# Value passes one head group at a time over zero-padded keys, and the last two batches exchanged in the seven products

## Chip, cores and metric

One core of a Trainium2 chip. The metric is device time in microseconds (us) of one execution of the whole kernel. A core has TensorE (PE, matmuls; its weight loads are shown as PEld), VectorE (DVE), ScalarE (ACT), GpSimd (POOL, which issues the input loads here) and SyncE (SP, which issues most stores).

## What is computed

Attention over 8 batches with 12 heads, 448 tokens and a head dimension of 64; its output, as 3584 rows of 768, goes through two matrices with SiLU between them.

```python
scores = scale * np.matmul(q, k.transpose(0, 1, 3, 2))
attn = np.exp(scores - max); attn = attn / sum
attn_out = np.matmul(attn, v)
x = attn_out.transpose(0, 2, 1, 3).reshape(B * S, H * D)   # 3584 x 768
h = x @ w_in                                               # 768 x 2048
g = h * (1.0 / (1.0 + np.exp(-h)))
out = g @ w_out                                            # 2048 x 768
```

## The kernel before

**Units and pairs.** The 12 heads are worked on in groups of 4 (HG). A unit is one group of one batch; batch 0 is cut into two pieces of the queries, so there are 27 units, 0 to 26. Units 0 to 6 stand alone ("lone"). The other twenty form ten pairs (7 and 8, 9 and 10, ... 25 and 26). The 448 keys of a unit lie in four chunks (NCH = 4) of the 128 partitions. In a pair three chunks are full, and the fourth, half a chunk, is shared: the first unit ("low") has its last keys in partitions 0 to 63, the second ("high") in 64 to 127 of one buffer, E[(ns[0], 3)].

**A unit's way.** `scores` (L350) and `scores_rest` multiply keys and queries in row strips (tiles of 32 rows, `score`, L337); `expo` (L374) takes the exponential on ScalarE into buffers E (9 of them, NE). For a pair `add_e` (L385) adds three chunks into T on VectorE, and `attend_sums` (L416) makes the sums of both units in one PSUM bank. `attend` (L424) runs the value passes, part 1 and part 2 (even and odd columns of V), with `attend_mm` (L400) in column strips (tiles of 32 columns; four such matmuls run side by side). For a pair a part takes two banks at once, one for each unit: 24 matmuls over the full chunks, and 8 over the 64 rows of the shared chunk (`rest()`), in tiles of 64 rows. `inverse` (L461 to L475) turns the sums into reciprocals, transposed, and `norm` (L491) writes the normalized output to xT, which frees the bank. Of the PSUM, a ring "m" of 4 banks serves sums, value passes, first products and second products; a ring "s" of 2 serves scores.

**The two matrices.** For batches 0 to 5 `ffn1` (L503, tile h, helper `times`) multiplies by w_in, 6 matmuls for each of 16 slices f; ScalarE's tanh (L529) and VectorE's `gate` (L564) make G. If TensorE's last work was in column strips, `times` does its product in strips too (four matmuls of 32 columns for one of 128), which spares a change of tile shape. The second product runs on quads of 128-row blocks (qd), each in seven products of half size instead of eight (`product`, tile p; sums S on VectorE, L705; `take_copy` L776 and `take_sum` L782 write the output). The first two blocks are multiplied plainly (tile o).

**The last two batches**, 6 and 7 (PB = 6), go through w_in together, in seven products for each f (`pair_product`, L652, tile f). They need four combinations of x (`combine_x`, L611, tile sx) and eight of w_in (`combine_w_in`, L629, tile tw), in buffers that were E's or V's. Product 1 is the first half of row 0 with w_in itself, product 2 its second half, product 5 takes sx_1, the sum of both halves of row 1, with tw_1; product 6 takes sx_2, 7 sx_3, 3 sx_4, and 4 the second half of row 1. Row 0 is batch 6, row 1 batch 7. ScalarE copies (L674) and VectorE adds (L678) gather the results, and ScalarE's Silu (L685) writes G.

**What sets the order.** All instructions are put in order by hand: class `Order` runs a planner at build time with estimated durations, and each engine's instructions are issued in the order in which the planner starts them. For VectorE and ScalarE `step` (L117) chooses among the ready operations the one with the smallest `at + op.bias`, its time of readiness plus a bias: -10 for `inverse` and `norm`, -4 for gates and output sums, -1 for add_e, 0 for S, 4 (SXB) for sx, 4 or 8 (TWB + f0) for tw, 20 for the transposes of keys and queries, 30 for combinations of w_out. On TensorE the loop at the end chooses among scores (`run_qk`), value passes (`run_av`, in the order of av_seq) and products (the list moe); where a score is due within AWAIT, a value pass is held back for it. POOL issues the loads in one fixed order: for each unit keys, queries, and four loads of V (`load_v`, L271), and w_in and w_out among the first. V has two buffers, one batch each; V's loads for a batch wait for the value passes of the batch two before.

Two small pieces that the change replaces:

```python
            4: (x[0, 1], sx_t.get(2), ALU.subtract),   # combine_x
...
        av_seq += [(ns, part) for part in range(3)]
```

Of the kernel before, what the change touches and what calls it, by code (L numbers as in the profile page):

```python
# [16 lines left out]
SWITCH = 0.094  # L17
# [12 lines left out]
def act(n):  # L30
    return n * 0.00087 + 0.13

# [45 lines left out]
class Order:  # L78
# [38 lines left out]
    def step(self):  # L117

        soon = []
        for eng in ("ACT", "DVE"):  # L120
# [45 lines left out]
def kernel(  # L166
# [37 lines left out]
    AWAIT = 0.8  # L204
    FAR = (NT * B // 4 - 3, NT * B // 4 - 1)
    TWB, SXB = 4, 4
# [59 lines left out]
    def load_v(b, hg0, hg1, x):  # L266
# [3 lines left out]
        first, count = X_TOK[form(b, hg0)][x]  # L270
# [315 lines left out]
    def old_buffer(name, home, cols):  # L586

        if home == "V":
            t = sb.tile([128, NH, NCH, D], FP16, name=name, tag="V", bufs=2)
            t = t.rearrange("p h c d -> p (h c d)")  # L590
        else:
# [25 lines left out]
    def combine_w_in(m, f0):  # L617
        if (m, f0) not in tw_t:
            made = old_buffer(f"tw_{m}_{f0}", W_HOME.get((m, f0), "E"), 512)
# [11 lines left out]
    W_HOME = {(1, 0): "V"}  # L631
    PBANK = {1: "A", 6: "A", 7: "A", 4: "A", 2: "B", 5: "C", 3: "C"}

    def pair_product(f, m):
# [6 lines left out]
        x = {(r, i): x3(PB + r, 3 * i) for r in range(2) for i in range(2)}  # L641
        lo, at = f // 4 * 4, slice(128 * (f % 4), 128 * (f % 4 + 1))
        a, w = {
            1: (x[0, 0], w_in_part(0, 0, f, f + 1)),
            2: (x[0, 1], w_in_part(1, 0, f, f + 1)),
            3: (sx_t.get(4), w_in_part(1, 1, f, f + 1)),
        }.get(m, (None, None))
        if a is None:
            i = {4: 4, 5: 1, 6: 2, 7: 3}[m]
            a, w = x[1, 1] if m == 4 else sx_t[i], tw_t[(i, lo)][:, :, at]  # L650
        for c in range(3):
            nc.tensor.matmul(  # L652
                out=pp_t[(f, PBANK[m])],
                lhsT=w[:, c, :],
                rhs=a[:, c, :],
                start=(c == 0 and m in (1, 2, 5)),
                stop=(c == 2),
                skip_group_check=True,
# [25 lines left out]
    def silu(f, r, x):  # L684
        nc.scalar.activation(  # L685
            out=G[:, f, S * r : S * (r + 1)],
# [260 lines left out]
    pair_todo = [(m, f0) for f0 in (0, 4) for m in (1, 2, 3, 4)]  # L947

    def plan_pair():
        while pair_todo and not od.pool:  # L950
            m, f0 = pair_todo[0]
            if (m, f0) in W_HOME:
                if not v_ring.can(1, od.now):
                    return
                v_ring.take()
            elif (m - 1, f0) not in W_HOME:
                if qk_seq or not e_ring.can(1, od.now):
                    return
                e_ring.take()
            pair_todo.pop(0)  # L960
            pair_w[(m, f0)] = od.add(
                Op(
                    "DVE",
                    0.98,
                    lambda m=m, f0=f0: combine_w_in(m, f0),
                    [pair_w[(k, f0)] for k in {2: (1,), 4: (2,)}.get(m, ())],
                    TWB + f0,
                )
            )

    def queue_pair():
        xs = {(r, c): x_op[(PB + r, c, 0)] for r in range(2) for c in range(NDC)}
        v_ring.take()
        e_ring.take(2)
        od.add(
            Op(
                "ACT",
                2.7,
# [590 lines left out]
```

## Time and profile before

Runs: 397.7, 398.45, 398.64 us, median 398.45. The profiled execution took 398.49 us.

| | us |
|---|---|
| profiled execution, its time | 398.49 |
| its span, first to last instruction | 396.7 |
| TensorE busy | 385.3 |
| VectorE busy | 275.1 |
| ScalarE busy | 252.7 |
| POOL busy | 83.7 |
| mean granted TensorE clock | 0.996 |

The span is the time from the first to the last instruction of any engine; the rest of the time lies around it. Busy times overlap. An engine's idle time before an instruction is put down to the engine or DMA whose signal came last ("issue": nothing that the profile shows). In rows of the timeline the first two numbers are the start in the span and the duration; consecutive equal instructions are merged, and a matmul's duration includes its way through the array, so that the next one starts before it ends. "128*32" is the tile, rows by columns. PEclk is the share of the TensorE clock that was granted.

### The profile page before, as it was taken

To read this page: it belongs to the slowest core of one execution; us is meant where nothing else is said; L and a number is where in the kernel's file an instruction comes from. 1 tells how busy PE (TensorE), PEld (TensorE's weight loads), DVE (VectorE), ACT (ScalarE), POOL (GpSimd) and SP (SyncE) were. 2 spreads that over 40 slices of the span, in tenths; PEclk is the share of its full clock that TensorE was granted. 3 is DMA by queue.
4 is the path that set the end of the run, shared out by engine and by line. 5 is a ranking of instruction groups with operands and counts; after the bars stand their busy time and mean duration, and the time that the engine had idled before them with its cause. 6 is when DMAs were issued, how large, how long until landed. Compare 5 with 4: busy or idle time off the path is not lost.

```text
span 396.7 us, 10765 instructions
## 1 busy us (share of the span) xinstructions
PE 385.3 (97%) x4429; PEld 202.3 (51%) x4429; DVE 275.1 (69%) x570; ACT 252.7 (64%) x399; POOL 83.7 (21%) x153
## 2 busy tenths in 40 slices
PE   8998999999999999999999999999999969999995
PEld 6666775444455445544445444444445524555663
DVE  2475776999985489457988469787899584456441
ACT  4986985696862883159675396867867237892120
POOL 7532547206001430024200614041000000000000
PEclk9999999999999999999999999999999989999999
DMA  7999999909033943173603667274000320001333
GB/s 113 204 209 210 159 185 170 184 17 138 5 88 81 132 56 59 49 135 51 96 7 84 109 106 104 36 128 71 2 2 22 89 53 0 0 2 30 92 99 101
DMA packets 35362, 34.54 MB, mean 87 GB/s; under 512 B 11376, under 2 KB 33776, under 8 KB 35312
## 3 DMA queue, kind: packets, MB, share of 16 engines
q0 software_dynamic: 24784, 22.82, 38.5%
q1 hardware_dynamic: 9952, 10.33, 9.7%
q8 instruction: 35, 0.57, 0.6%
q10 hardware_dynamic: 576, 0.69, 0.5%
q14 instruction: 15, 0.12, 0.1%
HBM read 45.61 MB, written 11.01 MB: 143 GB/s over the span
## 4 chain that ended last, share of the span: by engine, by line
PE 96%; DVE 1%; DMA 1%; issue 1%; ACT 0%; DVEq 0%; POOLq 0%
PE p L503 30%; PE h L503 29%; PE s L337 13%; PE a L400 11%; PE f L652 8%; PE o L503 3%; PE a L416 2%; DMA rk<-in_k_dram 1%; PE z L1474 1%; DVE xT L491 0%; DVE p L678 0%; ACT E L374 0%; DVE sx L611 0%; DVE KT L306 0%; ACT u L674 0%
## 5 line engine op out<-in xcount | busy, mean ns | idle before, releaser
L374 ACT ACTIVATE E<-s 128x896 f16<-128x896 f32 (+1 forms) x172 | 149.4, 914 | 31.4 <-PE s L337 29.7
L503 PE MATMUL h<-xT,w_in_t 128*128 128x448 f16 (+3 forms) x1122 | 119.0, 322 | 1.7 <-issue 1.7
L503 PEld LDWEIGHTS <-w_in_t 128*32 128x32 f16 (+1 forms) x1122 | 63.3, 97 | 53.7 <-issue 15.9
L529 ACT ACTIVATE th<-h 128x448 f16<-128x448 f32 (+1 forms) x112 | 54.5, 493 | 30.4 <-PE h L503 21.9
L564 DVE SCALAR_TENSOR_TENSOR G<-th,h 128x448 f16<-128x448 f16 (+2 forms) x112 | 55.5, 509 | 19.3 <-ACT th L529 16.9
L776 ACT COPY ost<-p 128x384 f32<-128x384 f32 x52 | 25.0, 481 | 65.5 <-PE p L503 62.0
L271 POOL DMA_DIRECT2D V<-in_v_dram x88 | 48.6, 573 | 75.9 <-PE a L400 62.1
L503 PEld LDWEIGHTS <-G 128*128 128x128 f16 (+1 forms) x580 | 42.9, 98 | 32.5 <-issue 5.6
L337 PE MATMUL s<-rq,KT 32*128 32x448 f16 (+4 forms) x768 | 50.6, 337 | 0.9 <-DVE rq L324 0.5
L503 PE MATMUL p<-w_out_t,G 128*128 128x384 f16 (+1 forms) x328 | 49.2, 326 | 0.0
L503 PEld LDWEIGHTS <-S 128*128 128x128 f16 (+1 forms) x456 | 30.1, 97 | 22.3 <-issue 3.1
L400 PE MATMUL a<-E,V 128*32 128x448 f16 (+3 forms) x864 | 40.1, 334 | 0.0
L503 PE MATMUL p<-D,S 128*128 128x384 f16 (+1 forms) x232 | 37.0, 326 | 0.0
L256 POOL DMA_DIRECT2D rq<-in_q_dram x27 | 15.2, 564 | 103.3 <-PE s L337 78.5
L491 DVE SCALAR_TENSOR_TENSOR xT<-a,rdn 128x448 f16<-128x448 f32 (+1 forms) x54 | 28.7, 567 | 10.7 <-PE a L400 9.9
L782 DVE TENSOR_TENSOR ost<-p,ost 128x384 f32<-128x384 f32 x39 | 21.5, 553 | 20.4 <-PE p L503 15.1
L337 PEld LDWEIGHTS <-KT 32*128 32x128 f16 (+2 forms) x864 | 17.4, 98 | 28.7 <-issue 26.0
L385 DVE TENSOR_TENSOR T<-T,E 128x1792 f16<-128x1792 f16 x20 | 21.8, 1089 | 13.7 <-ACT E L374 13.6
L400 PEld LDWEIGHTS <-V 128*32 128x32 f16 (+2 forms) x864 | 17.6, 95 | 20.4 <-issue 13.2
L385 DVE TENSOR_TENSOR T<-E,E 128x1792 f16<-128x1792 f16 x20 | 21.7, 1087 | 4.9 <-ACT E L374 4.9
L652 PE MATMUL f<-sx,tw 128*128 128x448 f16 x72 | 18.3, 381 | 3.3 <-DVE sx L611 3.2
L306 DVE STREAM_TRANSPOSE KT<-rk 128x256 f32<-128x256 f32 (+3 forms) x48 | 16.7, 385 | 6.3 <-DMA rk<-in_k_dram 6.1
(67 smaller groups left out, 323.0 us busy)
## 6 DMA issues: line engine op xcount, KB each, us to landing
out_dram<-ost SPq DMA_DIRECT2D x194, 48.0 KB, 1.7
rk<-in_k_dram POOLq DMA_DIRECT2D x24, 224.0 KB, 5.2
rq<-in_q_dram POOLq DMA_DIRECT2D x21, 224.0 KB, 5.4
w_in_t<-in_moe_w_in_dram POOLq DMA_DIRECT2D x6, 512.0 KB, 11.1
w_out_t<-in_moe_w_out_dram POOLq DMA_DIRECT2D x4, 768.0 KB, 13.7
V<-in_v_dram POOLq DMA_DIRECT2D x43, 64.0 KB, 3.8
V<-in_v_dram POOLq DMA_DIRECT2D x40, 48.0 KB, 3.8
out_dram<-ost SPq DMA_DIRECT2D x8, 96.0 KB, 2.1
```

Source lines behind the costliest of these rows:

```text
L271: nc.gpsimd.dma_start(out=VT[b][32 * x : 32 * (x + 1), hs, 0:count, :], in_=v[b, hs].rearrange("h (i g) d -> i h g d", g=TPP)[:, :, first ...
L337: nc.tensor.matmul(out=pS[p0 : p0 + 32 * (x1 - x0), h % 2, at : at + nq], lhsT=KT[(b, hg)][32 * h : 32 * (h + 1), c, x0:x1, :, e], rhs=QT[ ...
L374: nc.scalar.activation(out=E[(n, w)][0:kr, 2 * y : 2 * y + 2, 0:nk], in_=pS_t[(n, w, y)][0:kr, :, 0:nk], func=AF.Exp, scale=attn_scale,)
L385: nc.vector.tensor_tensor(out=T[n], in0=T[n] if step else E[(n, 0)], in1=E[(n, step + 1)], op=ALU.add,)
L400: nc.tensor.matmul(out=a[32 * h : 32 * (h + 1), 0:nq], lhsT=w, rhs=e[k0:k1, h, at : at + nq], start=start, stop=stop,)
L491: nc.vector.scalar_tensor_tensor(out=x3(b, cc)[:, cc % 3, 32 * g0 : 32 * g1], in0=acc[(n, part)][:, 0:nq], scalar=0.5, in1=rdn_t[n].rearra ...
L503: nc.tensor.matmul(out=out[i : i + cut], lhsT=w[:, i : i + cut], rhs=x, start=start, stop=stop, skip_group_check=True,)
L529: nc.scalar.activation(out=th, in_=h_t[(b, f, t0)][:, 0 : t1 - t0], func=AF.Tanh)
L564: nc.vector.scalar_tensor_tensor(out=dst[:, f, at + lo : at + hi], in0=th_t[(b, f, t0)][:, lo - t0 : hi - t0], scalar=1.0, in1=h_t[(b, f, ...
L652: nc.tensor.matmul(out=pp_t[(f, PBANK[m])], lhsT=w[:, c, :], rhs=a[:, c, :], start=(c == 0 and m in (1, 2, 5)), stop=(c == 2), skip_group_ ...
L776: nc.scalar.copy(out=ost(qd, *OUT[m]), in_=bank(qd, BANK[m]))
L782: nc.vector.tensor_tensor(out=t, in0=bank(qd, BANK[m]), in1=t, op=ALU.add)
```

## The change

- **Value passes.** `attend` now does one unit and one part at a time, in one bank, with four chunks of 128 rows. The shared chunk is read whole, with both units' keys, and V holds zeros in the half that is not the unit's: `load_v` sets this half of chunk 3 to zero on POOL ahead of the first of the four loads (20 such memsets). av_seq lists the passes as part 1 and 2 of the first unit, then of the second.
- **Roles of the last two batches.** Row 0 of the seven products is batch 7, row 1 batch 6 (`pair_half`, `silu`'s place in G, the gates' entries). `queue_pair` is called after part 1 of the last unit instead of after its part 2. The combinations are queued by `plan_pair` once every first product of batch 5 is placed, each with a home of its own (HOME): sx_1 and sx_2 in xT's buffers, sx_3 and sx_4 in E's. `pair_product` may run in strips. The load of Silu's table is queued by `plan_silu`.
- **VectorE's and ScalarE's choice** is by rank first: bias -9 or less, then up to 35, then above, and by time and bias within a rank. TWB becomes 40, so the combinations of w_in come last.
- AWAIT becomes 0. A norm's reciprocals may be 0.9 late for a pass instead of 1.2. The first products of batch 0 do not use strips any more.

```diff
+def rank(op):
+    return (op.bias > -9) + (op.bias > 35)
...
-                elif best is None or at + op.bias < best[0]:
-                    best = (at + op.bias, op)
+                elif best is None or (rank(op), at + op.bias) < best[0]:
+                    best = ((rank(op), at + op.bias), op)
...
-    AWAIT = 0.8
+    AWAIT = 0.0
     FAR = (NT * B // 4 - 3, NT * B // 4 - 1)
-    TWB, SXB = 4, 4
+    TWB, SXB = 40, 4
...
-        first, count = X_TOK[form(b, hg0)][x]
+        kind = form(b, hg0)
+        if x == 0 and kind != "lone":
+            lo = 64 if kind == "low" else 0
+            nc.gpsimd.memset(VT[b][lo : lo + 64, hs, NCH - 1, :], 0.0)
+        first, count = X_TOK[kind][x]
...
-    def attend(ns, part):
-        made = []
-        lone = len(ns) == 1
-        if part == 0 and not lone:
+    def attend(ns, part, n):
+        if part == 0 and len(ns) == 2:
             attend_sums(ns)
             return
-        for n in ns:
-            a = ps.tile([128, 512], FP32, name=f"a_{n}_{part}", tag="m", bufs=4)
-            made.append(a)
-            acc[(n, part)] = a
-
-        def rest():
+        acc[(n, part)] = ps.tile([128, 512], FP32, name=f"a_{n}_{part}", tag="m", bufs=4)
+        for c in range(NCH):
+            e = E[(ns[0] if c == NCH - 1 else n, c // per_burst(n))]
             for h in range(HG):
-                for i, n in enumerate(ns):
-                    attend_mm(
-                        made[i], n, part, 3, h, 64 * i, 64 * (i + 1), E[(ns[0], 3)],
-                        part == 2, part == 1,
-                    )
-
-        if not lone and part == 2:
-            rest()
-        for i, n in enumerate(ns):
-            for c in range(NCH if lone else NCH - 1):
-                for h in range(HG):
-                    attend_mm(
-                        made[i], n, part, c, h, 0, rows_of(n, c), E[(n, c // per_burst(n))],
-                        c == 0 and (lone or part == 1),
-                        c == NCH - (1 if lone else 2) and (lone or part == 2),
-                    )
-        if not lone and part == 1:
-            rest()
+                attend_mm(
+                    acc[(n, part)], n, part, c, h, 0, rows_of(n, c), e, c == 0, c == NCH - 1
+                )
 
     def inverse(ns, step, i=0):
         g0, g1 = units[ns[0]][2:]
...
+    def pair_half(r, i):
+        return x3(B - 1 - r, 3 * i)
+
     def combine_x(m):
-        if m < 4:
-            made = old_buffer(f"sx_{m}", "V" if m == 3 else "E", S)
-            for i, t in enumerate(made):
-                sx_t[m + i] = t
-        x = {(r, i): x3(PB + r, 3 * i) for r in range(2) for i in range(2)}
+        sx_t[m] = old_buffer(f"sx_{m}", HOME[("x", m)], S)[0]
         a, b, op = {
-            1: (x[1, 0], x[1, 1], ALU.add),
-            2: (sx_t.get(1), x[0, 0], ALU.subtract),
-            3: (x[0, 0], x[1, 0], ALU.subtract),
-            4: (x[0, 1], sx_t.get(2), ALU.subtract),
-        }[m]
+            1: lambda: (pair_half(1, 0), pair_half(1, 1), ALU.add),
+            2: lambda: (sx_t[1], pair_half(0, 0), ALU.subtract),
+            3: lambda: (pair_half(0, 0), pair_half(1, 0), ALU.subtract),
+            4: lambda: (pair_half(0, 1), sx_t[2], ALU.subtract),
+        }[m]()
         nc.vector.tensor_tensor(out=sx_t[m], in0=a, in1=b, op=op)
...
-    W_HOME = {(1, 0): "V"}
+    HOME = {
+        (0, 1): "V", (0, 2): None, ("x", 1): "x", ("x", 2): "x", (0, 3): "E", ("x", 3): "E",
+        (0, 4): "E", ("x", 4): "E", (4, 1): "V", (4, 2): None, (4, 3): "E", (4, 4): "E",
+    }
     PBANK = {1: "A", 6: "A", 7: "A", 4: "A", 2: "B", 5: "C", 3: "C"}
 
-    def pair_product(f, m):
...
         nc.scalar.activation(
-            out=G[:, f, S * r : S * (r + 1)],
+            out=G[:, f, S * (1 - r) : S * (2 - r)],
...
             def run(f=f):
-                strips = od.mode == "cols" and bool(qk_seq or av_seq)
+                strips = b > 0 and od.mode == "cols" and bool(qk_seq or av_seq)
                 op = Op("PE", NDC * mm(t1 - t0), lambda: ffn1(b, f, t0, t1, strips), tail=PE_OUT)
...
     pair_w, pair_x = {}, {}
-    pair_todo = [(m, f0) for f0 in (0, 4) for m in (1, 2, 3, 4)]
+    pair_todo = []
+
+    def xs(r, c):
+        return x_op.get((B - 1 - r, c, 0))
...
+        if "go" not in pair_w:
+            if od.pool or ffn1_left[PB - 1] or (PB - 1, 0) not in x_left:
+                return
+            pair_w["go"] = None
+            pair_todo.extend(HOME)
+        shut = set()
+        for kind, m in list(pair_todo):
+            home = HOME[(kind, m)]
+            mine = pair_x if kind == "x" else pair_w
+            made = [(m,) if kind == "x" else (m, kind)]
...
+            ring = {"V": v_ring, "E": e_ring}.get(home)
+            if None in made or home in shut or (home == "E" and qk_seq):
+                shut.add(home or kind)
+                continue
+            if ring is not None:
+                if not ring.can(1, od.now):
+                    shut.add(home)
+                    continue
+                ring.take()
+            pair_todo.remove((kind, m))
+            if kind == "x":
+                pair_x[m] = od.add(
+                    Op("DVE", 0.9, lambda m=m: combine_x(m), made, SXB)
                 )
+            else:
+                pair_w[(m, kind)] = od.add(
+                    Op("DVE", 0.98, lambda m=m, f0=kind: combine_w_in(m, f0), made, TWB + kind)
+                )
...
+    def plan_silu():
+        made = [g_op.get((PB - 1, f)) for f in range(NFF)]
+        if None not in made and not qk_seq and "silu" not in pair_w:
+            pair_w["silu"] = od.add(
+                Op("ACT", 2.7, first_silu, [x for y in made for x in y], -5)
...
-            g_op.setdefault((PB + r, f + HF * j), []).append(done[(j, r)])
+            g_op.setdefault((B - 1 - r, f + HF * j), []).append(done[(j, r)])
...
-                made = [xs[0, c] for c in (range(3, NDC) if m == 2 else range(3))]
+                made = [xs(0, c) for c in (range(3, NDC) if m == 2 else range(3))]
+                if f > 1 and m in (1, 5):
+                    made.append(xs(0, NDC - 1) and xs(0, 0))
                 i = {5: 1, 6: 2, 7: 3, 3: 4}.get(m)
                 if i:
-                    made.append(pair_x[i])
+                    made.append(pair_x.get(i))
...
-            queue_pair()
...
-        av_seq += [(ns, part) for part in range(3)]
+        av_seq += [(ns, 0, ns[0])] + [(ns, part, n) for n in ns for part in (1, 2)]
...
+                deps += [(x, 0.9) for x in rdn_op.get(n, [None])]
+        at, m = when(deps), m_ring.when(1)
+        return None if at is None or m is None else max(at, m)
...
-        ns, part = av_seq.pop(0)
-        b, hg, g0, g1 = units[ns[-1]]
+        ns, part, n = av_seq.pop(0)
...
+        m_ring.take()
...
-        od.on_pe(op, "rest cols" if two and part == 2 else "cols")
-        if two and part:
-            od.mode = ("rest cols", "cols")[part - 1]
+        od.on_pe(op, "cols")
...
+        if part == 1 and n == NU - 1:
+            queue_pair()
```

More of the change, by code (lines that the diff above doesn't have):

```diff
@@ L590, in old_buffer @@
             t = t.rearrange("p h c d -> p (h c d)")
+        elif home == "x":
+            return [sb.tile([128, 3, S], FP16, name=name, tag="xT", bufs=NX3)]
         else:
@@ L649, in pair_product @@
             i = {4: 4, 5: 1, 6: 2, 7: 3}[m]
-            a, w = x[1, 1] if m == 4 else sx_t[i], tw_t[(i, lo)][:, :, at]
+            a, w = lambda: pair_half(1, 1) if m == 4 else sx_t[i], tw_t[(i, lo)][:, :, at]
         for c in range(3):
[L652 to L658, printed above, removed]
+            times(
+                pp_t[(f, PBANK[m])],
+                w[:, c, :],
+                a()[:, c, :],
+                c == 0 and m in (1, 2, 5),
+                c == 2,
+                strips,
             )
@@ L969, in plan_pair @@
+    def plan_silu():
[3 more added lines that the diff above has]
+                Op("ACT", 2.7, first_silu, [x for y in made for x in y], -5)
             )
     def queue_pair():
[L972 to L978, printed above, removed]
-                first_silu,
-                [x for f in range(NFF) for x in g_op[(PB - 1, f)]],
-                -5,
-            )
-        )
@@ L996, in queue_pair_f @@
-    def queue_pair_f(f, xs):
+            queue_pair_f(f)
+    def queue_pair_f(f):
         done, lo = {}, f // 4 * 4
@@ L1027, in run @@
                     ring.take(need)
-                od.on_pe(op, "full")
+                od.on_pe(op, "cols" if strips else "full")
                 done[m] = op
@@ L1060, in deps @@
                 made += [(done.get(x), 9.0) for x in {2: ["p"], 3: ["u"]}.get(m, [])]
-                return made + (free(0) if m == 1 else free(1) if m == 5 else [])
+                return made + (free(1) if m == 1 else free(0) if m == 5 else [])
             moe.append((deps, int(m in (2, 5)), run, rings))
@@ L1415, in then @@
             def then(at):
-                for _ in range(7 if two else NCH // per_burst(ns[0])):
+                for _ in range((3 + (n == ns[1])) if two else NCH // per_burst(n)):
                     e_ring.give(at)
-                if any(units[n][1] == NG - 1 and units[n][3] == TPP for n in ns):
+                if hg == NG - 1 and g1 == TPP:
                     v_ring.give(at)
@@ L1429, in run_av @@
         else:
-            for n in ns:
-                after_av(n, part, op, nq)
+            after_av(n, part, op, nq)
     def after_sums(ns, op, nq):
@@ L1487 @@
             moe_i, moe_next = moe_ready()
-            av_data["at"] = None
             qk, av = qk_at(), av_at()
-            wait = av_data["at"]
-            if wait is not None and wait <= od.now - 1000 and not (av is not None and av <= od.now):
-                moe_i, moe_next = moe_ready(0)
-                soon.append(min([x for x in m_ring.free if x>od.now] or [od.now+0.1]))
             near = qk_seq and units[qk_seq[0][0][0]][0] == 0 and qk is not None
```

96 lines of the change are left out of this document (31 added, 65 removed).

## The prediction

> **What bounds the kernel now.** I read the page's busy shares first, then its chain, then the list of TensorE's waits, and last the timeline around each wait.
>
> ```profile
> span 396.7 us, 10765 instructions
> ...
> PE 385.3 (97%) x4429; PEld 202.3 (51%) x4429; DVE 275.1 (69%) x570; ACT 252.7 (64%) x399; POOL 83.7 (21%) x153
> ...
> PE 96%; DVE 1%; DMA 1%; issue 1%; ACT 0%; DVEq 0%; POOLq 0%
> ```
>
> TensorE's matmuls are 96% of the chain that ends last, so an edit counts if it changes the number of matmul time slots, the number of times the array changes its tile shape, or TensorE's waits. The list of its waits has six entries. Four are 1.0 us or less and stand in the first 28 us, which the change leaves as they are. The other two:
>
> ```profile
> PE f L652 <- DVE sx L611: 3.2, 1, 3.2
> PE h L503 <- issue: 1.7, 1, 1.7
> ```
>
> The first stands where attention ends and the seven products of the last two batches begin (PE's and DVE's rows of the timeline, start and duration in us):
>
> ```profile
> 318.79 2.44 PE L652 MATMUL f<-xT,w_in_t 128*128 128x448 f16 x12
> 321.43 1.15 DVE L491 SCALAR_TENSOR_TENSOR xT<-a,rdn 128x448 f16<-128x448 f32 x2
> 323.56 0.84 DVE L611 TENSOR_TENSOR sx<-xT,xT 128x1344 f16<-128x1344 f16 x1
> 324.46 5.48 PE L652 MATMUL f<-sx,tw 128*128 128x448 f16 x18 [3.22 <-DVE sx L611]
> 329.77 0.73 PE L652 MATMUL f<-sx,w_in_t 128*128 128x448 f16 x3
> 330.34 0.73 PE L652 MATMUL f<-sx,tw 128*128 128x448 f16 x3
> ```
>
> Four products that need no sum run until 321.2. The next (m = 5) needs sx_1, the sum of both halves of batch 7, and batch 7's last piece is normalized only at 321.4 to 322.5. The wait is 3.22 us, and there is a second loss behind it. From 324.46 to 329.77 eighteen matmuls take 5.31 us. Three of the same shape take 330.34 - 329.77 = 0.567, so 0.189 each, and eighteen should take 3.41. The missing 1.90 us is in the granted clock (PEclk) of the table by stretches:
>
> ```profile
> core 0: us, PE busy (x) PEld busy (x) DVE busy (x) ACT busy (x) POOL busy (x), PEclk, DMA share, GB/s
> 318.00:321.00 3.00, 3.00 (x32) 1.34 (x24) 2.08 (x3) 1.06 (x2) 0.00 (x0) 1.00 0.28 69
> 321.00:324.00 3.00, 0.24 (x2) 0.00 (x0) 3.00 (x6) 0.86 (x2) 0.00 (x0) 1.00 0.32 84
> 324.00:327.00 3.00, 2.54 (x9) 1.14 (x10) 3.00 (x5) 1.31 (x3) 0.00 (x0) 0.67 0.00 0
> 327.00:330.00 3.00, 2.95 (x13) 1.26 (x12) 0.68 (x1) 1.60 (x3) 0.00 (x0) 0.77 0.00 0
> ```
>
> The clock falls to 0.67 and 0.77 right behind the gap and is 1.00 on both sides. The Trainium skill, TensorE: Matmul & The Clock Gate, Part 1, puts the halving of the clock down to an idle window of about 3.4 us and its return to a busy window of that length; by this the loss would be half of 3.4, so an estimated 1.7 instead of 1.90 us, and the sum below would be 0.2 higher.
>
> The second wait is early, in the batch-0 products, which run in strips of 32 columns:
>
> ```profile
> 31.07 0.94 PE L400 MATMUL a<-E,V 128*32 128x224 f16 x32
> 31.84 0.27 PE L503 MATMUL h<-xT,w_in_t 128*32 128x224 f16 x4
> 33.85 1.24 PE L503 MATMUL h<-xT,w_in_t 128*32 128x224 f16 x44 [1.74 <-issue]
> ```
>
> It falls within one product, behind 4 of 48 matmuls, and names no releaser. In this stretch (31 to 33 us) the DMA engines are full and one packet of TensorE's own instructions is among the traffic:
>
> ```profile
> q8 instruction: 1, 0.02, 3.0%
> ```
>
> I read the gap as TensorE having run out of instructions while the next block of them stood in line behind the loads.
>
> **The change part by part.** The base is the profiled execution: 398.49 us with a span of 396.7, so 1.79 lie around the span; the median of the runs is 398.45, the same within 0.04.
>
> *Value passes.* Before, a pair of head groups takes 7 slots of 0.189 us a part for both groups: 24 matmuls of 128 rows run four at a time (6 slots) and the 8 short ones of 64 rows run eight at a time (1 slot). Afterwards each group has its own pass of 16 matmuls over 128 rows, 4 slots, so 8 a part. Ten pairs, two parts: 20 x 0.189 = **+3.78**.
>
> *Changes of tile shape.* The price is read from a repeating stretch:
>
> ```profile
> 79.67 0.57 PE L337 MATMUL s<-rq,KT 32*128 32x448 f16 x8
> 80.18 2.44 PE L503 MATMUL h<-xT,w_in_t 128*128 128x448 f16 x12
> 82.56 0.58 PE L337 MATMUL s<-rq,KT 32*128 32x448 f16 x8
> ```
>
> From 79.67 to 82.56 are 2.89 us for 2 + 12 slots (2.65), so 0.24 for two changes; the neighbouring cycle, from 76.79, gives 0.23. I take 0.115 each. In the order of instructions of the two programs the shape changes 234 times before and 206 times after: the 30 into and out of the 64-row value tiles go, and two others come in. 28 x 0.115 = **-3.22**. So the passes nearly pay for themselves. As a check, two parts back to back:
>
> ```profile
> 95.20 3.07 PE L400 MATMUL a<-E,V 128*32 128x448 f16 x64
> 98.09 1.31 PE L503 MATMUL h<-xT,w_in_t 128*32 128x448 f16 x24
> ```
>
> 2.89 us for 14 slots (2.65) and 0.24 for the two inner changes; 16 slots without them are 3.03. Parts that stand alone gain on the next product, which may stay in strips.
>
> *Roles swapped.* sx_1 is now made of batch 6, which is normalized two units ahead of the end. In the new order all 14 products of quads 8 and 9 stand between the last value pass and the first of the seven products; eight matmuls of them take 374.08 - 372.78 = 1.30 us, so 18.2 us of cover for combinations of 0.85 (sx) and 0.95 us (tw). The 3.22 us wait goes, **-3.22**, and with it the slow clock, **-1.90**.
>
> *Batch 0 without strips.* The same slots with a quarter of the instructions. From the waiting product on, the instructions that TensorE had in hand now last through two whole products (2 x 6 x 0.098 = 1.2 us; thirty take 2.98 us at 41.98), a score burst of 0.5 and about three changes of shape: 31.84 + 0.1 + 2.1, about 34.0, when the block (landed by 33.85) is there. Before, this place (the start of h_0_3) was reached at 35.53; I take **-1.63**. The bounds are 0 and -1.74.
>
> *Memsets.* The 20 memsets of 64 x 256 elements stand on POOL ahead of V's loads. No row has one of this size: the lower bound is POOL's memset of one element, 0.10 us, the upper VectorE's 1.09 for an add of 1792 elements; I take 0.3, nearer the small one, 6 us in all. POOL is busy 83.7 of 396.7 us, and TensorE has no wait on V's loads in the list: cost nothing. Uncovered, it would be one memset for each wait, 20 x 0.1 to 1.09 = 2 to 22 us. Behind a memset queue V's four loads and the next keys and queries. The one place where that is tight: the last piece of w_out (POOL sits idle for it until 61.54) is needed near 63.2 afterwards, against 65.4 before; two memsets move its issue by 0.6 and leave about 1 us.
>
> *VectorE by rank, combinations late.* The same operations. The risk is that they bunch: in the 18.2 us behind attention I count 16 sums at 0.34, 6 adds at 0.56, 3 sx at 0.85, 8 tw at 0.9 and 2 gates at 0.7, together 20.0 us (two sums in a row take 0.75 with 0.42 each, so 0.34 from start to start). Three tw (2.7 us) are needed only by the fifth slice, so it just fits. For this and for bank waits between passes I add **+0.3**: the bounds are 0 and 3 (the 20.0 us entirely in the way, with 1 us for a bank).
>
> The sum: 398.49 + 3.78 - 3.22 - 3.22 - 1.90 - 1.63 + 0.3 = **392.6 us**.
>
> **The rivals.**
>
> 1. *The early gap stays.* The cause is not instructions, or their block comes as much later. For it: its row shows "issue", no cause. Against it: it falls in mid-product, where no instruction waits on another engine. It gives 392.6 + 1.63 = 394.2. The Trainium skill, Runtime: NRT & Kernel Launch, Instruction fetch mechanics, holds that fetching is hidden because instructions issue slower than they arrive, and that TensorE holds 2048 of them; by this rule the gap is no fetch and stays. No row here shows the buffer's size.
>
> 2. *The wait moves into the 14 products.* VectorE comes late with the sums of quads 8 and 9, having normalized the last passes and made sx first. For it: the 20.0 us above. Against it: the closing products (355 to 392 us) have the same sums per product without one wait. Three us and a slow clock behind them (1.90 at most) give 392.3 + 3 to 4.9 = 395.3 to 397.2; I say 396.
>
> 3. *Slower: VectorE's normalizing chain is late at each pair.* One bank per pass lets TensorE reach the second, third and fourth pass sooner, and each needs a bank that a norm frees. The chain behind the sums is 0.65 + 0.33 + 1.17 (two transposes) and 0.62 for a norm, 2.77 us; if an add of 1.09 is ahead of it, 3.86. Between a pair's sums and its first pass stand mostly two products and a score burst, 2.8 us, and two passes (1.5) find banks free: 4.3, so it is hidden. At two pairs of the ten (units 11 and 21) a single product (1.3) stands there, and it isn't. It must cost more than 398.49 + 1.2 - 392.6 = 7.1 us to be slower, 0.71 at each of ten pairs; a full add at each gives 10.9, so 403.5 us.
>
> 4. *The gains come in part and the change washes out*: half of rival 3 and the late w_out, 5 to 6 us, 398.
>
> **How the numbers follow.** Forecast 0.58, with a range of its own of 391.2 (changes of shape at 0.13 us, -0.4; no new waits, -0.3; the early gap wholly gone, -0.1; the spread of the runs shown, about -0.5) to 393.8; rival 1 0.14 (394.2), rival 2 0.11 (396), rival 3 0.10, rival 4 0.07. A difference under 0.3% (1.2 us) can't be told from none here. Faster takes the first three: 0.83; same 0.07; slower 0.10. For eight in ten the range runs from 391.2 over rivals 1 and 2 to 397.
>
> **What would show it.** Right: no wait on sx in TensorE's list and a granted clock of 1.00 throughout behind attention; two passes of 16 value matmuls in about 1.5 us; the first 36 us without a wait of 1.7. Wrong: a wait of "a" on VectorE's xT that recurs at each pair (rival 3), one of "p" on S near 300 to 320 us (rival 2), or value passes of more than 0.78 us each in a row.

## The result, and the profile after

The changed kernel takes 394.47 us (median of four runs), beside 398.43 for the kernel before. The ratio is 0.9898, with a 95% interval of 0.9874 to 0.9922, so about 4 us of the forecast 5.9 came. Medians here and below are of all runs; one disturbed run each of four kernels (after; full tiles in batch 0; clock kept up; the fastest without the exchange) is left out of the ratios, and without it these four medians are 394.01, 407.12, 397.17 and 393.97. The profiled execution took 394.92 us.

The page of the kernel after, its first lines and the shares of the chain that ended last:

```profile
span 393.1 us, 10622 instructions
...
PE 384.6 (98%) x4345; PEld 206.3 (52%) x4345; DVE 274.4 (70%) x570; ACT 253.9 (65%) x399; POOL 89.0 (23%) x173
...
PE 95%; DVE 1%; DMA 1%; ACT 1%; issue 1%; DVEq 0%; POOLq 0%
```

TensorE still bounds the kernel. Its five longest waits (engine, line, releaser; us in total, times, longest):

```profile
PE z L1458 <- DVE zeros L227: 1.0, 1, 1.0
PE a L408 <- DVE xT L479: 1.0, 1, 1.0
PE a L408 <- issue: 0.8, 2, 0.5
PE s L345 <- DVE rq L332: 0.5, 1, 0.5
PE p L491 <- DVE ost L773: 0.4, 1, 0.4
```

Both waits that the prediction set out to remove are gone: 3.2 us on sx, and 1.7 us in batch 0. A wait of 1.0 on xT is new, and a small one of a product on an output tile; the other three stand ahead of the first product of batch 0. The clock behind attention, in the table by stretches of the kernel after:

```profile
core 0: us, PE busy (x) PEld busy (x) DVE busy (x) ACT busy (x) POOL busy (x), PEclk, DMA share, GB/s
321.00:324.00 3.00, 3.00 (x18) 1.56 (x16) 2.33 (x3) 2.24 (x6) 0.00 (x0) 1.00 0.39 102
324.00:327.00 3.00, 3.00 (x18) 1.54 (x17) 1.78 (x3) 2.50 (x7) 0.00 (x0) 1.00 0.41 109
```

It is 1.00, where it was 0.67 and 0.77. The early stage (PE's rows of the timeline, kernel after) has no gap within a product any more:

```profile
32.15 0.95 PE L408 MATMUL a<-E,V 128*32 128x224 f16 x32
33.03 1.32 PE L491 MATMUL h<-xT,w_in_t 128*128 128x224 f16 x12
34.29 0.57 PE L345 MATMUL s<-rq,KT 32*128 32x448 f16 x8
```

The new wait, in the timeline of the kernel after, TensorE's and VectorE's rows:

```profile
117.16 1.47 PE L491 MATMUL p<-w_out_t,S 128*32 128x384 f16 x32
118.56 0.58 PE L345 MATMUL s<-rq,KT 32*128 32x448 f16 x8
118.68 0.76 DVE L696 TENSOR_TENSOR S<-G,S 128x512 f16<-128x512 f16 x2 [2.28 <-PE p L491]
119.36 0.62 DVE L479 SCALAR_TENSOR_TENSOR xT<-a,rdn 128x448 f16<-128x448 f32 x1
...
120.13 0.94 PE L408 MATMUL a<-E,V 128*32 128x448 f16 x16 [0.99 <-DVE xT L479]
```

VectorE stands idle for 2.28 us ahead of an S sum, whose buffer is free only when a product (117.16 to 118.6) has read it. Behind that sum in VectorE's order stands a norm whose value pass had ended at 117.3 us and whose bank TensorE's next value pass needs. So the pass waits 0.99 us at the pair of units 11 and 12. Ahead of the 0.44 us wait on an output tile, at 176 us, VectorE had likewise stood idle, for 3.18 us, before an S sum that needed a buffer.

**A measure without the start.** The first product of batch 0 (tile h) starts at 29.49 us in the profile before and at 30.57 after, and between 29.46 and 30.60 in the others, while the loads come in. To compare profiles I take this start off the span: 396.7 - 29.49 = 367.2 before, 393.1 - 30.57 = 362.5 after, a difference of 4.7 us. The last column of the next table is this number.

| kernel | median, us | ratio to before, 95% interval | span behind the first product |
|---|---|---|---|
| before | 398.4 to 398.7 | 1 | 367.2 |
| after | 394.47 | 0.9898 (0.9874 to 0.9922) | 362.5 |
| after, once more | 394.31 | 0.9894 (0.9870 to 0.9918) | 362.5 |
| before, full tiles in batch 0 | 407.28 | 1.0196 (1.0161 to 1.0231) | 375.9 |
| before, clock kept up | 397.19 | 0.9969 (0.9951 to 0.9987) | 365.5 |
| before, value passes alone | 395.12 | 0.9914 (0.9888 to 0.9941) | 363.4 |
| before, exchange alone | 395.14 | 0.9925 (0.9899 to 0.9951) | 363.5 |
| after, old value passes | 393.61 | 0.9882 (0.9859 to 0.9904) | 362.0 |
| after, 64-row tiles | 401.98 | 1.0090 (1.0070 to 1.0110) | 370.3 |
| after, strips kept | 395.95 | 0.9939 (0.9915 to 0.9963) | 364.3 |
| after, no rank | 398.07 | 0.9976 (0.9958 to 0.9995) | 365.6 |
| after, four S buffers | 392.59 | 0.9847 (0.9816 to 0.9878) | 361.0 |
| passes and full tiles alone | 393.97 | 0.9886 (0.9857 to 0.9916) | 362.4 |
| the fastest without the exchange | 394.26 | 0.9889 (0.9865 to 0.9912) | 361.6 |

### The profile page after: what moved, and what is told of

Read it like the earlier page. It is cut to its first block, busy times and chain, and to the rows that moved or that the text cites. A ratio compares the mean times of both kernels' runs of the same rounds, so it can differ in the third digit from the quotient of the medians.

```text
span 393.1 us, 10622 instructions
## 1 busy us (share of the span) xinstructions
PE 384.6 (98%) x4345; PEld 206.3 (52%) x4345; DVE 274.4 (70%) x570; ACT 253.9 (65%) x399; POOL 89.0 (23%) x173
## 4 chain that ended last, share of the span: by engine, by line
PE 95%; DVE 1%; DMA 1%; ACT 1%; issue 1%; DVEq 0%; POOLq 0%
PE p L491 30%; PE h L491 29%; PE s L345 12%; PE a L408 11%; PE f L491 8%; PE o L491 3%; PE a L424 2%; DMA rk<-in_k_dram 1%; PE z L1458 1%; ACT E L382 1%; DVE KT L314 0%; DVE S L696 0%; DVE rq L332 0%; DVE xT L479 0%; ACT ost L767 0%
## 5 line engine op out<-in xcount | busy, mean ns | idle before, releaser
L491 PE MATMUL h<-xT,w_in_t 128*32 128x448 f16 (+2 forms) x1086 | 117.1, 336 | 0.0
L491 PEld LDWEIGHTS <-w_in_t 128*128 128x128 f16 (+1 forms) x1158 | 71.1, 97 | 56.4 <-issue 11.5
L408 PE MATMUL a<-E,V 128*32 128x448 f16 (+2 forms) x864 | 42.5, 333 | 1.3 <-DVE xT L479 1.0
L479 DVE SCALAR_TENSOR_TENSOR xT<-a,rdn 128x448 f16<-128x448 f32 (+1 forms) x54 | 30.4, 568 | 6.4 <-PE a L408 4.5
L408 PEld LDWEIGHTS <-V 128*32 128x32 f16 (+1 forms) x864 | 20.8, 96 | 20.1 <-issue 8.8
L491 PE MATMUL p<-D,G 128*32 128x384 f16 (+1 forms) x176 | 19.1, 326 | 0.4 <-DVE ost L773 0.4
```

What stands on the lines that cost most here:

```text
L408: nc.tensor.matmul(out=a[32 * h : 32 * (h + 1), 0:nq], lhsT=w, rhs=e[k0:k1, h, at : at + nq], start=start, stop=stop,)
L479: nc.vector.scalar_tensor_tensor(out=x3(b, cc)[:, cc % 3, 32 * g0 : 32 * g1], in0=acc[(n, part)][:, 0:nq], scalar=0.5, in1=rdn_t[n].rearra ...
L491: nc.tensor.matmul(out=out[i : i + cut], lhsT=w[:, i : i + cut], rhs=x, start=start, stop=stop, skip_group_check=True,)
```

## The experiments

**1. Full tiles in batch 0, alone.** On the kernel before:

```diff
-                strips = od.mode == "cols" and bool(qk_seq or av_seq)
+                strips = b > 0 and od.mode == "cols" and bool(qk_seq or av_seq)
```

> The kernel before with one edit: batch 0's first products do not use strips. Theory A (the early 1.74 us gap is TensorE out of instructions, and fewer instructions close it): 1.6 us faster, 396.8 us, no wait above 0.6 us in the first 60 us. Rival B (the gap is only handed on: the shortage comes back as smaller gaps near 22, 28 and 53 us, as the changed kernel's profile suggests with 0.3, 0.5 and 0.4): 0.3 us faster, 398.1.

It took 407.28 us, 8.6 more than the 398.73 of the kernel before beside it; neither theory expected that. The early gap is gone, but the planner, given other durations early on, put the score bursts of units 11 and 12 next to each other with nothing between them. PE's rows of the timeline of this kernel, and the table by stretches:

```profile
122.16 0.37 PE L337 MATMUL s<-rq,KT 32*128 32x448 f16 x2 [0.82 <-ACT E L374]
122.97 0.74 PE L337 MATMUL s<-rq,KT 32*128 32x448 f16 x6 [0.44 <-ACT E L374]
124.36 0.56 PE L337 MATMUL s<-rq,KT 32*128 32x448 f16 x2 [0.65 <-ACT E L374]
...
131.35 2.65 PE L400 MATMUL a<-E,V 128*32 128x448 f16 x32
```

```profile
110.00:120.00 10.00, 10.00 (x114) 5.46 (x112) 3.42 (x6) 1.97 (x4) 0.00 (x0) 1.00 0.31 80
120.00:130.00 10.00, 6.61 (x55) 1.58 (x52) 4.65 (x7) 7.99 (x10) 0.55 (x1) 0.66 0.23 60
130.00:140.00 10.00, 10.00 (x134) 3.95 (x133) 6.66 (x13) 5.96 (x8) 4.18 (x8) 0.83 0.43 54
```

Each burst waits for ScalarE to free a bank, and TensorE is busy for 6.61 of 10 us. The 0.66 is a mean: asked of shorter stretches, the table gives 1.00 up to 123.22 us and 0.50 from there to 133.46, although no single wait is longer than 0.82. So this run says nothing of what the edit is worth; its place has to be measured in a kernel whose order stays (experiment 8).

**2. The slow clock alone.** On the kernel before, fifteen matmuls of zeros into a free bank while sx_1 is waited for; the wait itself stays:

```diff
+        if f == 0 and m == 5:
+            for _ in range(15):
+                nc.tensor.matmul(
+                    out=spare["t"][:, 1, 0:S], lhsT=zeros, rhs=x[0, 0][:, 0, :], start=True, stop=True
+                )
```

> The kernel before with 15 extra matmuls of 448 columns (2.84 us by 0.189 each), whose results nothing reads, in the 3.22 us wait for sx_1. The wait for sx_1 stays. Theory A (idle time lowers the granted clock, and that cost 1.90 us): granted clock 1.00 from 324 to 330 us, 1.9 us faster, 396.5 us. Rival B (the eighteen matmuls behind the wait are slow for another reason, such as their weights coming from tw): no faster, 398.4 us, and they still take 5.3 us.

Measured: ratio 0.9969 (1.2 us), and 1.7 us in the profiles (367.2 to 365.5), less than the forecast 1.9. In this kernel's timeline and table:

```profile
321.68 3.00 PE L656 MATMUL f<-xT,zeros 128*128 128x448 f16 x15
325.07 3.79 PE L660 MATMUL f<-sx,tw 128*128 128x448 f16 x18 [0.39 <-DVE sx L611]
328.70 0.73 PE L660 MATMUL f<-sx,w_in_t 128*128 128x448 f16 x3
```

```profile
324.00:327.00 3.00, 2.62 (x15) 1.17 (x14) 3.00 (x5) 1.94 (x5) 0.00 (x0) 1.00 0.06 16
327.00:330.00 3.00, 2.95 (x16) 1.43 (x15) 2.32 (x4) 1.95 (x4) 0.00 (x0) 1.00 0.00 0
```

The clock stays at 1.00, and the eighteen matmuls behind the wait take 328.70 - 325.07 = 3.63 us instead of 5.31: 1.68 us of the loss was the clock, and the other 0.22 of the 1.90 stays at full clock. In the profile before, the table gives a clock of 0.50 for 325.00 to 328.41 us and 1.00 on both sides: half of 3.41 us is lost, 1.71. The Trainium skill, TensorE: Matmul & The Clock Gate, Part 1, would have put it at an estimated 1.7, which agrees. The ratio is smaller than the profiles' difference because not every execution of the kernel before has this slow clock: three of the seventeen beside this run show a mean clock of 0.999 or 1.00 and take 397.1 to 397.4 us, as the filled kernel does, and the others 0.991 to 0.996 and 398.3 to 400.0.

**3. The old value passes in the changed kernel**, with two banks a part and no memsets.

```diff
-        av_seq += [(ns, 0, ns[0])] + [(ns, part, n) for n in ns for part in (1, 2)]
+        av_seq += [(ns, part) for part in range(3)]
...
-            nc.gpsimd.memset(VT[b][lo : lo + 64, hs, NCH - 1, :], 0.0)
```

> The changed kernel with the value passes as before (two banks a part, 64-row tiles for the shared chunk, no memsets, no zeros in V). Theory A (passes only trade slots for shape changes): 20 slots fewer is -3.78 us, 239 shape changes instead of 206 is +3.80, so 394.5 us, the same as the changed kernel; without its wait of 1.0 us at 119 us, 393.5. Rival B (passes by single banks also fill waits that pairs of banks leave): 396 us or more, with waits of value passes for banks in TensorE's list. Rival C (the passes cost more than their slots, by late norms): below 393 us.

Ratio 0.9882, a little below the changed kernel's 0.9894; the profiles differ by 0.5 us the same way. The intervals overlap, so the passes of the change cost about half a microsecond here or nothing. Theory A's second figure, 393.5, is met, and its reason too: the waits of 1.0 us on xT and 0.4 on an output tile are absent here, and one of 0.4 on tw is there. Behind the first product TensorE is busy for 357.02 us in this kernel and for 356.76 in the changed one, so the new passes themselves are 0.3 us the cheaper, and what they cost is the wait.

**4. The price of a change of shape.** In the changed kernel the shared chunk is read in tiles of 64 rows again, one unit at a time. The slots stay the same, the zeros go, and the shape changes 275 times instead of 206:

```diff
-                    acc[(n, part)], n, part, c, h, 0, rows_of(n, c), e, c == 0, c == NCH - 1
+                    acc[(n, part)], n, part, c, h, *rows_in(ns, n, c), e, c == 0, c == NCH - 1
```

> The changed kernel, same order and same slots, but the shared chunk is read in tiles of the unit's own 64 rows, so V needs no zeros and has no memsets. 275 shape changes instead of 206. Theory A (a change of tile shape costs 0.115 us): 69 x 0.115 = 7.9 us slower than the changed kernel, 402.4 us. Rival B (the gaps at shape changes belong to the score bursts and products themselves): 394.5 us or, if the memsets cost anything, less.

It took 401.98 us: (401.98 - 394.3) / 69 = 0.11 us a change. One wait of 1.0 us for a load of V has come and the one of 1.0 on xT is gone, so the waits cancel. The 0.115 of the prediction stands.

**5. The changed kernel once more**, as a control.

> The changed kernel itself once more, as the control for the three runs beside it, because a kernel with the old value passes has come out at 393.6 us and the changed one, on another chip and day, at 394.5. Both theories: 394.5 us within 0.5, ratio to before 0.990. If it comes out under 393.9, the difference between those two kernels was a difference of chips, and the value passes cost nothing either way; if at 394.3 or more, they cost some 0.8 us.

394.31 us, ratio 0.9894; the span behind the first product is the same as in the first profile to 0.1 us.

**6. The value passes alone**, on the kernel before: `attend`, `load_v` and av_seq as in the change, all else as before.

> The kernel before with the value passes alone: one bank a pass, zeros in V, the passes in the new order; roles, strips and VectorE's order as before. Shape changes 234 to 202, slots 20 x 0.189 more. Theory A (as predicted, the passes pay for themselves and the waits on sx_1 and in batch 0 stay): 398.5 + 3.78 - 32 x 0.115 = 398.6 us, ratio 1.000. Rival B (one bank a pass makes VectorE's norms late at many pairs): over 400. Rival C (the passes are what made the changed kernel faster): under 396.

395.12 us, inside rival C's band: better than A by 3.5. The list of waits of this kernel says why:

```profile
PE h L487 <- issue: 1.7, 1, 1.7
PE p L487 <- DVE xT L475: 1.2, 1, 1.2
```

There is no wait on sx, although the roles are the old ones. The end of attention in its timeline:

```profile
298.00 3.36 PE L404 MATMUL a<-E,V 128*32 128x448 f16 x64
302.52 2.76 PE L487 MATMUL p<-w_out_t,G 128*128 128x384 f16 x16 [1.17 <-DVE xT L475]
...
319.42 1.46 PE L487 MATMUL p<-D,G 128*128 128x384 f16 x8
320.72 0.73 PE L636 MATMUL f<-xT,w_in_t 128*128 128x448 f16 x3
321.28 0.73 PE L636 MATMUL f<-sx,tw 128*128 128x448 f16 x3
```

With passes for one unit the planner ends attention at 301.4 us and puts all fourteen products of quads 8 and 9 behind it; in the kernel before, the last value pass ended at 318.9. That order alone gives sx_1 its cover. The price is a wait of 1.17 us on a norm, which stands behind two combinations of w_in.

**7. The exchange alone**, on the kernel before: `pair_half`, HOME, `plan_pair`, `queue_pair` and `plan_silu` as in the change; passes, strips, choice and AWAIT as before.

> The kernel before with the last two batches exchanged alone (the combinations in homes of their own, no wait on sx_1); value passes, strips in batch 0, VectorE's choice and AWAIT as before. Theory A (the whole gain is this wait and the slow clock behind it): 398.5 - 3.2 - 1.9 = 393.3 us, ratio 0.987, with the 1.7 us gap of batch 0 still in the list of waits, so the other parts of the change bring nothing together. Rival B (the gap of batch 0 must go too for the whole gain): 394.5 to 395.

395.14 us, 1.8 above A and 0.1 above B's band. The wait on sx is gone here too (attention still ends at 319.7, but sx_1 is made of batch 6). 3.7 of the 5.1 us come in the profile: the closing products now wait twice for an output tile, 1.1 us in all.

```profile
PE h L507 <- issue: 1.7, 1, 1.7
PE p L507 <- ACT ost L783: 1.1, 2, 0.6
```

So either edit by itself removes the wait and the slow clock (the granted clock is 1.00 from 318 to 330 us in both), and this gain can't be had twice.

**8. Strips kept**: the changed kernel with the edit of experiment 1 undone.

> The changed kernel with strips in batch 0 again; TensorE's order is otherwise the same, with 204 shape changes for 206. Theory A (as predicted, the early gap is instructions that come late, and full tiles took it away): the gap of 1.7 us is back near 32 us and the time rises by up to 1.6, to 395.7 to 396.1 us, 1.2 to 1.6 above the control. Theory B (formed on the profile after: what the full tiles saved there was lost again in smaller gaps up to 54 us): within 0.4 us of the control, with other gaps marked issue.

395.95 us, 1.64 above the control, with no overlap of the runs (395.7 to 396.5 against 393.5 to 394.5). TensorE's rows:

```profile
32.34 0.27 PE L491 MATMUL h<-xT,w_in_t 128*32 128x224 f16 x4
34.34 1.24 PE L491 MATMUL h<-xT,w_in_t 128*32 128x224 f16 x44 [1.74 <-issue]
```

The gap is back behind the same four matmuls with the same length, 1.74, and theory B falls. Between 31 and 35 us the DMA queues of this kernel show one packet of instructions among the loads:

```profile
q0 software_dynamic: 503, 0.82, 111.9%
q8 instruction: 1, 0.02, 1.4%
```

The Trainium skill, Runtime: NRT & Kernel Launch, Instruction fetch mechanics, calls fetching hidden; whether the 1.74 us here speak against it is open, since the gap comes and goes with the number of TensorE's instructions and stands at one fixed place in the program, but no run shows that it is a fetch. The trace's records of queue 8 put the landing of this packet 1.30 to 1.47 us ahead of the end of the gap in the five kernels with strips in batch 0, while the gap is 1.74 in each of them; a gap that ended with this landing would vary with it. Strips bring the gap and full tiles remove it; what TensorE waits for in it stays open.

**9. Four S buffers.** The changed kernel with one more buffer for sums, and two output buffers fewer for the space:

```diff
-    NSG, NOST = 3, 7
+    NSG, NOST = 4, 5
```

> The changed kernel with four S buffers for three (and five output buffers for seven, for the space). The S sum that stood ahead of unit 11's norm at 118.68 us then needs no product to end first. Theory A (the 0.99 us wait of a value pass on xT is a norm queued behind an S sum that waits for a buffer): that wait is gone, perhaps also the 0.4 of the product at 174.5, and the time is 392.4 to 393.2 us, 1.1 to 1.9 under the changed kernel. Rival (rival 3's own mechanism, VectorE's chain of transposes and norms is too long behind a pair's sums when a single product stands there): the wait stays at 0.7 or more and the time within 0.4 us of 394.3. Rival C: fewer output buffers bring waits of products on output tiles, 0.4 us or more each.

392.59 us, the fastest of all and inside A's band: 1.7 under the control, 1.5 in the profiles. The waits of this kernel over 0.2 us are three, all ahead of the first product; none is on xT, and none on an output tile, as rival C had it:

```profile
PE z L1458 <- DVE zeros L227: 1.0, 1, 1.0
PE s L345 <- DVE rq L332: 0.9, 1, 0.9
PE s L345 <- ACT E L382: 0.4, 1, 0.4
```

At the pair of units 11 and 12 the norm now comes before the end of the product and not behind it:

```profile
116.26 1.47 PE L491 MATMUL p<-w_out_t,S 128*32 128x384 f16 x32
116.48 0.63 DVE L479 SCALAR_TENSOR_TENSOR xT<-a,rdn 128x448 f16<-128x448 f32 x1 [0.18 <-PE a L408]
117.66 0.57 PE L345 MATMUL s<-rq,KT 32*128 32x448 f16 x8
118.17 0.94 PE L408 MATMUL a<-E,V 128*32 128x448 f16 x16
```

So the sum in front of the norm was the cause, and not the length of VectorE's chain of transposes and norms, whose operations are the same here.

**10. Passes and full tiles alone**: the kernel of experiment 6 with the edit of experiment 1.

> The kernel before with the value passes and with batch 0 without strips, and nothing else: no exchange of the last two batches, no rank, AWAIT 0.8. It differs from the run of the passes alone (395.1 us) by the strips, and by what the planner makes of them later; its score bursts are as many and as far apart as before. Theory A (the passes take the wait on sx_1 away by themselves, the full tiles 1.6 us more, and the exchange is not needed): 393.2 to 393.9 us, ratio 0.987 to 0.989, no wait on sx in the list. Rival B (the exchange is needed once the order shifts): a wait on sx of 1 us or more behind attention and 395 us or more.

393.97 us, 0.07 above A's band and clear of B: no wait on sx, and the 1.2 us on xT as in experiment 6. These two parts give as much as the whole change.

**11. No rank.**

```diff
-    return (op.bias > -9) + (op.bias > 35)
+    return 0
...
-    TWB, SXB = 40, 4
+    TWB, SXB = 4, 4
```

> The changed kernel with VectorE's old choice: no rank, and the combinations of w_in at a bias of 4 for 40. TensorE's order differs only from the last value passes on. Theory A (20.0 us of VectorE's work just fit into the 18.2 behind attention and what the rank orders has slack): 394.3 us within 0.4, no wait over 0.5 between 300 and 325 us. Rival B (the rank is what keeps the combinations of w_in from standing ahead of the sums of quads 8 and 9): a wait of a product on S of 1 to 3 us there, 395.3 to 397.

398.07 us, 3.8 above the control (3.1 in the profiles): nearly the whole gain is lost, more than either theory gave. The twelve executions fall into two groups: six with a mean clock of 0.997 to 1.00 take 396.9 to 397.8 us, the profiled one among them, and six with 0.994 to 0.996 take 398.3 to 398.6. The timeline of this kernel shows where:

```profile
299.98 3.56 DVE L618 TENSOR_TENSOR tw<-w_in_t 128x1536 f16<-128x1536 f16 x4
303.45 0.85 DVE L600 TENSOR_TENSOR sx<-xT,xT 128x1344 f16<-128x1344 f16 x1
304.22 0.42 DVE L696 TENSOR_TENSOR S<-G 128x512 f16<-128x512 f16 x1
304.55 0.62 DVE L479 SCALAR_TENSOR_TENSOR xT<-a,rdn 128x448 f16<-128x448 f32 x1
```

```profile
301.22 1.46 PE L491 MATMUL p<-w_out_t,G 128*128 128x384 f16 x8
305.23 2.77 PE L491 MATMUL p<-w_out_t,G 128*128 128x384 f16 x16 [2.55 <-DVE xT L479]
```

Four combinations of w_in, one of x and one sum go ahead of the last norm, 4.6 us in all, and the second product needs the bank that this norm frees. It is rival B's ordering, but the wait is on a bank and not on S. The profile has the clock at 1.00, so its 3.1 us are waits; that the other six executions lose about 1 us more to a slow clock behind this wait is likely, but they have no trace.

**12. The fastest version without the exchange**: passes, full tiles, rank and four S buffers on the kernel before.

> The fastest version so far (four S buffers, 392.6 us, ratio 0.985) without the exchange of the last two batches: the kernel before with the value passes, full tiles in batch 0, the rank with the combinations of w_in last, four S buffers and five output buffers. Theory A (the wait on sx_1 is gone because attention ends ahead of quads 8 and 9, and the rank keeps VectorE's norms ahead of the combinations; the exchange brings nothing then): 392.3 to 393.1 us, ratio 0.984 to 0.986, no wait on sx or xT of 1 us behind 290 us. Rival B (batch 7 as row 1 puts sx_1 behind the last norm, and sx_1 comes late again): a wait on sx or tw of 0.8 us or more near 318 us, 393.5 to 395.

394.26 us, ratio 0.9889, with five runs from 392.9 to 395.0: neither band is met as a whole. There is no wait on sx or xT, as A says. Scores wait three times, 1.8 us in all, for queries (rq), but all three stand ahead of the first product. Behind it this kernel is 0.6 us longer than the one with the exchange (361.6 against 361.0), and the intervals of the two ratios overlap, so whether the exchange still earns anything there stays open.

## Why the prediction came out as it did

Forecast 392.6 us, 5.9 under the profiled execution before; measured 394.47 and 394.31, 4.0 to 4.1 under the runs of before beside them. The direction held, and so did the wide range (391.2 to 397); the forecast's own range ended at 393.8, and the forecast was 1.7 to 1.9 us too low. The first rival's 394.2 fits the measured time, but that is chance: its mechanism, an early gap that stays, did not happen.

- **Value passes against changes of shape** (+3.78 and -3.22): both terms hold. A change of shape cost 0.11 us in experiment 4. Behind the first product TensorE is busy for 357.94 us before and 356.76 after, 1.18 less; 1.68 of that is the clock, which leaves +0.5 for passes and shapes, against +0.56 in the sum. (The half microsecond of experiment 3 is something else, the new wait.) What the sum did not have is that the passes change the planner's order. In experiment 6 that order alone took the wait on sx away.
- **Roles swapped** (-3.22 and -1.90): the size of the wait holds; of the 1.90 behind it 1.68 was the clock. The attribution holds only by half. The exchange removes the wait (experiment 7), and so do the passes (experiment 6). The wait could be removed only once, and the prediction rightly counted it once, in the order that both edits made together.
- **Batch 0 without strips** (-1.63): 1.64 in experiment 8. The first rival, that the gap stays, fell. The closeness is luck: the prediction's own working gives 35.53 - 34.04 = 1.49, not 1.63. That the block of instructions stood in line behind the loads, as the prediction read the gap, is not borne out by the packet's landing.
- **Memsets** (0.3 us each, hidden): they took 0.305, and TensorE waits for none of V's loads in the kernel after.

```profile
L277 POOL MEMSET V<- 64x256 f16 x20 | 6.1, 305 | 29.1 <-PE a L408 28.5
```

- **VectorE by rank, and bank waits** (+0.3): this is the term that failed. Behind attention it was right, the 20.0 us of work fit, but only because of the rank: without it 3.1 us come back in the profile and 3.8 in the median (experiment 11). The new waits stood elsewhere, 0.99 us at 119 us and 0.44 at 176, 1.4 us instead of 0.3; a fourth S buffer, which removes both, is worth 1.5 us in the profiles and 1.7 in the medians (experiment 9). The third rival had named units 11 and 21 as the two pairs without cover, and it struck at one of them. But it priced a norm behind an add of 1.09 us; what stood ahead of the norm was a sum of 0.76 that itself waited 2.28 us for a buffer. In an order written out by hand such a waiting instruction holds up everything behind it on its engine.
- The steps without the new waits come to 3.78 - 3.22 - 3.22 - 1.90 - 1.63 = -6.2. From 367.2 that gives 361.0 behind the first product, which is what the profile with four S buffers shows; with 1.4 us of waits it gives 362.4, against 362.5 in the kernel after. What is left of the error of 1.7 to 1.9 us, some 0.7, lies ahead of the first product, as far as the profiles show: the profile that the sum was made against had nearly the earliest start of all, 29.49 of 29.46 to 30.60 us, and the one after nearly the latest.

## What to carry to other kernels

A gain that hangs on one wait is counted once, however many edits remove it; to learn which one does, each is run alone. Where an engine's instructions are in a fixed order, ask of each instruction ahead of a critical one not how long it takes but what it waits for: a buffer more can be worth more than a shorter chain. And an edit that changes a planner's input is tested in a kernel whose order stays the same, since the planner's new order cost more than 8 us in one kernel here (experiment 1).

## What the hardware did that was not expected

- The clock did not need one long gap to fall. In experiment 1 it is at 0.50 from 123.22 to 133.46 us; in the 3.41 us ahead of that TensorE was busy for 2.05, with no single wait over 0.82. Matmuls in this stretch ran slow (2.65 us for 32 strips at 131.35, against 1.63 for the 32 at 134.44).
- The same gap does not always bring it. Over the runs beside all experiments, the kernel before, with its gap of 3.22 us, showed a mean clock of 0.997 or more in 12 of 55 executions (median 397.3 us), 0.995 or 0.996 in 31 (398.6) and 0.990 or 0.991 in 12 (399.8). The gap of 2.55 us in experiment 11 left the clock at 1.00 in the profiled execution, but six of the twelve executions of that kernel show 0.994 to 0.996. One profile of a kernel is therefore not enough to say that a gap is too short to matter.
- TensorE's early gap has the same length, 1.74 us, and the same place in the program in every kernel here that runs batch 0 in strips, and it is in none of the others.
